# Loading an output projection in 26, 5 and 1 rows instead of 21, 7, 3 and 1, the 26 into another buffer

## The chip, the cores and the metric

The kernel runs on one core of a Trainium2 chip. The core has five engines that run side by side, each with its own instructions in order: PE (matrix multiplication; PEld is its loading of weights), DVE and ACT (elementwise work), POOL, and SP, which here only issues DMA transfers. Transfers bring data from memory (HBM) into the on-chip memory SBUF, which has 128 partitions; PE writes its results to PSUM. The metric is the device time of one execution in microseconds (us), lower is better.

## The reference

Two independent decode steps of attention, A and B, whose results stand side by side in the output. Each has one query token, 32 query heads, 16 key/value heads (two query heads share one), 8192 cached keys, 128 elements a head and a model width of 576. A looks only at its last 2048 keys.

```python
def ref(x, k_cache, v_cache, wq, wo, W):             # A: W = 2048, B: W = 8192
    q = (x @ wq).reshape(B, Sq, Hq, Dh).transpose(0, 2, 1, 3)
    k = repeat(k_cache[:, :, Sk - W:, :], 2, axis=1)
    v = repeat(v_cache[:, :, Sk - W:, :], 2, axis=1)
    scores = einsum("bhqd,bhkd->bhqk", q, k) * Dh ** -0.5
    o = einsum("bhqk,bhkd->bhqd", softmax(scores), v)
    return o.transpose(0, 2, 1, 3).reshape(B, Sq, Hq * Dh) @ wo
out = concatenate([ref(A...), ref(B...)], axis=-1)   # 1152 numbers
```

The caches and the weights are bf16, 102.76 MB are read in all.

## The kernel before

**Order of the work.** The queries of A and B come first: wq of each is loaded and multiplied (`q_part`). Then five groups follow (`NG`): group 0 is the whole of A, groups 1 to 4 are four key/value heads of B each. In each group the keys arrive in two loads (`load_k`, the buffers `("k", 0)` and `("k", 1, ...)`, the first and second quarter of the SBUF tensor `slots`) and the values in one (`load_v`, `("v", 0..2)`, the other half of `slots`). PE turns the keys in eight units (`k_transpose`, line 496), into four PSUM banks. ACT and DVE copy each bank to the SBUF tensor `kt` (lines 506 and 509), which holds four units of 4096 elements per partition; unit u lies in place u mod 4. `k_scores` (line 521) multiplies a unit by the queries, two units behind the transposes. Softmax follows (`softmax_exp`, `softmax_transpose`), then the products with the values (`v_sums`, line 588).

In the last group PE also works out the weights by which the parts of each head are put together (`weights_top`, `weights_exp`, `weights_sum`, `combine`), and A's 4096 results stand ready before the last V sums start. After these, DVE keeps the last group's sums (`v_keep`, line 606), PE combines them (line 671) and DVE copies B's results into `opj` (line 676).

**The output projection.** wo has 4096 x 576 numbers: 32 rows of 576 for each of 128 partitions, so "a row" is here one row in every partition, 144 KB in all. The list `wo_loads` (line 769) says, for A (P = 0) and for B (P = 1), which rows come in which load, to where, and after which buffers are free. `load_wo` makes the load from an entry and `wo_part` (line 691) the matmuls: two per row for A (288 columns each), four per row for B (144 columns each), each of the four in its own strip of 32 columns of the array. All 32 rows of a projection add up in PSUM; `finish_out` copies the sum out and stores it, A's before B's.

**What orders the work.** Each operation names what it reads and writes; `Program.add` notes which earlier operations it must follow, and `emit` turns that into semaphore waits on the engine that runs it. On PE the five groups are a loop; on the other engines they are written out. All loads of slots are issued by SP (line 398 for wo and wq, 407 and 411 for keys, 422 and 427 for values) in program order: one that waits holds all behind it. So before the change SP issues, at the end, A's 32 rows (when the first part of the keys of group 4 has been turned), B's 21 rows (second part of the keys), B's 7 rows (after the last V sums, whose home they take), then 3 and 1 rows behind them, in the same home. The names `("w", 0)` and `("w", 1)` in those two entries are not used elsewhere: they are ordered by standing behind the 7 rows on SP.

PE works through A's 32 rows, then through B's parts in the order of the list, each after its load has landed.

## Time and profile before

| what | value |
|---|---|
| median of the runs | 245.51 us (245.44 to 245.77, 4 runs) |
| the profiled execution, its own time | 245.32 us |
| its span, first to last instruction | 243.8 us |
| read from memory | 102.76 MB, 421 GB/s over the span |
| busy time | PE 161.7 us, PEld 115.9, DVE 88.1, ACT 92.4, POOL 6.4 |
| granted TensorE clock, mean | 0.865 |
| wo of A: issued, landing after | 211.27 us, 19.7 us |
| wo of B, 21 rows: issued, landing after | 211.65 us, 26.5 us |
| wo of B, 7, 3 and 1 rows: landing after | 9.4, 10.1 and 10.0 us |

Times of a place in the profile are counted from the start of the span. "Landing after" is the time from the issue of a load to its last byte. The clock is the share of its full rate that PE was granted; it is 1.00 or 0.50 at any one time. The DMA share is the mean busy share of the core's 16 DMA engines.

### The profile page before, as it was taken

To read this page: it belongs to the slowest core of one execution; us is meant where nothing else is said; L and a number is where in the kernel's file an instruction comes from. 1 tells how busy PE (TensorE), PEld (TensorE's weight loads), DVE (VectorE), ACT (ScalarE), POOL (GpSimd) and SP (SyncE) were. 2 spreads that over 40 slices of the span, in tenths; PEclk is the share of its full clock that TensorE was granted. 3 is DMA by queue.
4 is the path that set the end of the run, shared out by engine and by line. 5 is a ranking of instruction groups with operands and counts; after the bars stand their busy time and mean duration, and the time that the engine had idled before them with its cause. 6 is when DMAs were issued, how large, how long until landed. Compare 5 with 4: busy or idle time off the path is not lost. (4 is left out here: it accounts for less than half of the span.)

```text
span 243.8 us, 5212 instructions
## 1 busy us (share of the span) xinstructions
PE 161.7 (66%) x2325; PEld 115.9 (48%) x2325; DVE 88.1 (36%) x152; ACT 92.4 (38%) x96; POOL 6.4 (3%) x33
## 2 busy tenths in 40 slices
PE   0007639948387995194999453999446699845964
PEld 0002238735236783143886221868222687535753
DVE  0001228854307454203656202555322255533130
ACT  2000017845306686101878300877500387630000
POOL 5000100000000000000000000000000000000000
PEclk9999958997859999657999759999858799977799
DMA  9999999999999999899999999999999999989994
GB/s 339 436 411 419 430 433 422 430 427 430 460 427 431 484 398 462 371 430 435 485 409 452 403 409 430 430 478 430 441 392 430 430 478 430 473 356 441 414 410 179
DMA packets 4064, 102.88 MB, mean 422 GB/s; under 512 B 596, under 2 KB 728, under 8 KB 984
## 3 DMA queue, kind: packets, MB, share of 16 engines
q1 hardware_dynamic: 3896, 102.76, 98.3%
q8 instruction: 6, 0.10, 0.2%
q10 hardware_dynamic: 160, 0.00, 0.0%
q14 instruction: 2, 0.02, 0.0%
HBM read 102.76 MB, written 0.00 MB: 421 GB/s over the span
## 5 line engine op out<-in xcount | busy, mean ns | idle before, releaser
L506 ACT ACTIVATE kt<-ktps 128x1024 bf16<-128x1024 bf16 x80 | 78.9, 1039 | 87.9 <-PE ktps L496 87.9
L496 PE MATMUL ktps<-ident,slots 128*128 128x128 bf16 x1280 | 83.3, 227 | 22.7 <-PEq L214 18.9
L496 PEld LDWEIGHTS ktps<-ident,slots 128*128 128x128 bf16 x1280 | 77.1, 102 | 38.7 <-issue 38.6
L509 DVE COPY kt<-ktps 128x1024 bf16<-128x1024 bf16 x80 | 60.7, 772 | 55.2 <-PE ktps L496 55.2
L588 PE MATMUL opsum<-slots,ptm 128*32 128x512 bf16 x320 | 28.4, 531 | 11.6 <-PEq L214 11.6
L521 PE MATMUL sacc<-kt,qst 128*32 128x512 bf16 x320 | 25.8, 398 | 2.2 <-PEq L214 2.2
L588 PEld LDWEIGHTS opsum<-slots,ptm 128*32 128x32 bf16 x320 | 13.9, 128 | 24.6 <-issue 22.3
L559 PE MATMUL misc<-ident,psb 128*128 128x128 bf16 x40 | 4.5, 283 | 15.8 <-PEq L214 15.8
L606 DVE TENSOR_TENSOR vtmp<-opsum,maskV 128x512 f32<-128x512 f32 x4 | 2.8, 691 | 31.9 <-PE opsum L588 31.9
L547 ACT ACTIVATE psb<-sacc,stat 128x2048 bf16<-128x2048 f32 x5 | 9.8, 1967 | 9.7 <-DVE stat L536 9.7
L559 PEld LDWEIGHTS misc<-ident,psb 128*128 128x128 bf16 x40 | 3.4, 126 | 18.2 <-issue 18.2
L438 PE MATMUL misc<-xnine,twice 64*128 64x18 bf16 x1 | 0.2, 171 | 17.8 <-DMA xnine<-in_B_x_dram 17.8
L566 DVE TENSOR_TENSOR ptm<-misc,maskP 128x1024 bf16<-128x1024 bf16 x5 | 3.5, 691 | 15.9 <-PE misc L559 15.9
L521 PEld LDWEIGHTS sacc<-kt,qst 128*32 128x32 bf16 x320 | 5.0, 94 | 8.4 <-issue 4.8
L438 PEld LDWEIGHTS misc<-xnine,twice 64*128 64x128 bf16 x1 | 0.1, 102 | 17.8 <-issue 17.8
L703 ACT ACTIVATE outsb<-ktps 64x144 bf16<-64x144 f32 x1 | 0.3, 288 | 21.5 <-PE ktps L691 21.5
L691 PE MATMUL ktps<-slots,opj 128*32 128x144 bf16 (+1 forms) x192 | 6.8, 247 | 2.3 <-DMA slots<-in_B_wo_dram 2.3
L462 ACT ACTIVATE qrow<-opsum 128x512 bf16<-128x512 f32 x1 | 0.6, 597 | 19.2 <-PE opsum L456 19.2
L691 PEld LDWEIGHTS ktps<-slots,opj 128*32 128x32 bf16 x192 | 5.2, 97 | 3.8 <-DMA slots<-in_B_wo_dram 3.2
L447 DVE TENSOR_SCALAR xpad<-misc,par 128x5 bf16<-128x5 f32 (+1 forms) x8 | 1.2, 227 | 13.5 <-PE misc L438 13.5
L481 POOL COPY qst<-qcol 128x32 bf16<-128x32 bf16 x8 | 1.7, 213 | 146.3 <-PE sacc L521 146.3
L534 DVE TENSOR_REDUCE stat<-sacc 128x1 f32<-128x512 f32 x5 | 3.5, 691 | 4.4 <-PE sacc L521 4.4
(76 smaller groups left out, 57.7 us busy)
## 6 DMA issues: line engine op xcount, KB each, us to landing
slots<-in_B_k_cache_dram SPq DMA_DIRECT2D x8, 4096.0 KB
slots<-in_A_k_cache_dram SPq DMA_DIRECT2D x4, 2048.0 KB
slots<-in_A_v_cache_dram SPq DMA_DIRECT2D x4, 2048.0 KB
slots<-in_A_wq_dram SPq DMA_DIRECT2D x1, 4608.0 KB, 13.6
slots<-in_B_wq_dram SPq DMA_DIRECT2D x1, 4608.0 KB, 23.8
slots<-in_A_wo_dram SPq DMA_DIRECT2D x1, 4608.0 KB, 19.7
slots<-in_B_wo_dram SPq DMA_DIRECT2D x1, 3024.0 KB, 26.5
slots<-in_B_wo_dram SPq DMA_DIRECT2D x1, 1008.0 KB, 9.4
```

Source lines behind the costliest of these rows:

```text
L481: return pool.tensor_copy(dst, src)
L496: ins = pe.matmul(ktps_bf[q][:, t * 128:(t + 1) * 128], lhsT=slots[:, o:o + 128], rhs=ident[:, :], start=True, stop=True, is_transpose=True)
L506: add("act", lambda act, src=src, dst=dst: act.activation(dst, src, ACT.Copy), reads=[("bank", q)], writes=[("kt", u % NKT, q)], tag="e%d% ...
L509: add("dve", lambda dve, src=src, dst=dst: dve.tensor_copy(dst, src), reads=[("bank", q)], writes=[("kt", u % NKT, q)], tag="e%d%d" % (u, q))
L521: ins = pe.matmul(sacc[32 * j:32 * j + 32, :], lhsT=qst[:, o:o + 32], rhs=rhs, start=(u == 0 and e == 0), stop=True, skip_group_check=True)
L534: add("dve", lambda dve: dve.tensor_reduce(st(C_M + g), sacc[:, :], AX.X, ALU.max), reads=[B_S], writes=[("st", C_M + g)], tag="max")
L547: return act.activation(dst, src, ACT.Exp, bias=st(C_NB + g), scale=SCALE, accum_out=st(C_L + g))
L559: ins = pe.matmul(dst[:, t * 128:(t + 1) * 128], lhsT=psb[:, o:o + 128], rhs=ident[:, :], start=True, stop=True, is_transpose=True)
L566: return dve.tensor_tensor(ptm[:, c * 1024:(c + 1) * 1024].rearrange("p (t y) -> p t y", t=8), dst.rearrange("p (t y) -> p t y", t=8), mas ...
L588: ins = pe.matmul(opsum[64 * j + 32 * x:64 * j + 32 * x + 32, :], lhsT=ptm[:, o:o + 32], rhs=v[:, at[0], at[1], :, :, b:b + 128], start=(n ...
L606: add("dve", lambda dve: dve.tensor_tensor(vtmp[:, :, :], src, by, ALU.mult), reads=[B_O, w], writes=["vtmp"], tag="keep")
L691: ins = pe.matmul(ktps[P + j // 2][32 * j:32 * j + 32, 0:w], lhsT=opj[:, P, at:at + 32], rhs=slots[:, o:o + w], start=(jj == 0), stop=(jj ...
```

## The change

B's wo comes in three loads instead of four. Its first 26 rows go to `kt`, and wait until all four units there have been read by the last scores; the next 5 go to where the 21 rows began, in the second keys' home; the last row follows them there. `load_wo` and `wo_part` take the tensor as an argument. A's load, the order of PE's matmuls and the stores are as they were.

```diff
+    ktw = kt[:, :, :].rearrange("p u y -> p (u y)")
...
-    def load_wo(P, lo, n, off, res):
-        load(slots[:, off:off + n * DM], lambda: wos[P].rearrange("(p j) n -> p (j n)", p=128)[:, lo * DM:(lo + n) * DM],
+    def load_wo(P, lo, n, tile, off, res):
+        load(tile[:, off:off + n * DM], lambda: wos[P].rearrange("(p j) n -> p (j n)", p=128)[:, lo * DM:(lo + n) * DM],
              res, "wo%d_%d" % (P, lo))
...
-                                    rhs=slots[:, o:o + w], start=(jj == 0), stop=(jj == HQ - 1))
+                                    rhs=tile[:, o:o + w], start=(jj == 0), stop=(jj == HQ - 1))
...
     wo_loads = [
-        (0, 0, 32, 0, [("k", 0), ("k", 1, 0)]),
-        (1, 0, 21, WQ_W, [("k", 1, 1)]),
-        (1, 21, 7, 2 * SLOT, [("v", 0), ("v", 1)]),
-        (1, 28, 3, 2 * SLOT + 7 * DM, [("w", 0)]),
-        (1, 31, 1, 2 * SLOT + 10 * DM, [("w", 1)])]
+        (0, 0, 32, slots, 0, [("k", 0), ("k", 1, 0)]),
+        (1, 0, 26, ktw, 0, [("kt", u, q) for u in range(NKT) for q in range(4)]),
+        (1, 26, 5, slots, WQ_W, [("k", 1, 1)]),
+        (1, 31, 1, slots, WQ_W + 5 * DM, [("w", 0)])]
```

## The prediction

> **What bounds the kernel now.** I read the chain of waits first, because it says what ended last. It ends in a wo load, the last rows of B's output projection, the copy out of PSUM and the store:

> ```profile
> 231.53 10.11 DMA slots<-in_B_wo_dram
> 241.64 0.04 issue
> 241.69 0.65 PE ktps L691 x16
> 242.35 0.30 DVE outsb L703
> ```

> Then the list of DMA issues, for how long each wo load took from its issue to its last byte:

> ```profile
> slots<-in_A_wo_dram SPq DMA_DIRECT2D x1, 4608.0 KB, 19.7
> slots<-in_B_wo_dram SPq DMA_DIRECT2D x1, 3024.0 KB, 26.5
> slots<-in_B_wo_dram SPq DMA_DIRECT2D x1, 1008.0 KB, 9.4
> slots<-in_B_wo_dram SPq DMA_DIRECT2D x1, 432.0 KB, 10.1
> slots<-in_B_wo_dram SPq DMA_DIRECT2D x1, 144.0 KB, 10.0
> ```

> The 144 KB load needs as long as the 1008 KB load: all five stand in one line and are served in the order of issue. So I asked for PE's timeline at the end (start, length, line, count, idle time before):

> ```profile
> 233.25 3.96 PE L691 MATMUL ktps<-slots,opj 128*32 128x288 bf16 x62
> 238.21 1.50 PE L691 MATMUL ktps<-slots,opj 128*32 128x144 bf16 x84 [0.99 <-DMA slots<-in_B_wo_dram]
> 240.62 0.62 PE L691 MATMUL ktps<-slots,opj 128*32 128x144 bf16 x28 [0.92 <-DMA slots<-in_B_wo_dram]
> 241.69 0.62 PE L691 MATMUL ktps<-slots,opj 128*32 128x144 bf16 x16 [0.44 <-DMA slots<-in_B_wo_dram]
> ```

> PE starts 0.05 us after a landing (241.64 to 241.69), so the 21, 7 and 3 rows land at 238.16, 240.57 and 241.64; the last row's four matmuls start at 242.05, so it lands at 242.00. A's wo lands at 211.27 + 19.7 = 231.0. PE waits for DMA before every part of B: bytes bound this stage.

> **The change, part by part.**

> *The wait that goes.* The 7, 3 and 1 rows were issued only after the last V sums, at 231.16 to 232. Did the DMA engines run dry meanwhile? In three windows (length; busy time and count of PE, PEld, DVE, ACT, POOL; PE clock; DMA share; GB/s) they did not:

> ```profile
> 228.00:231.00 3.00, 3.00 (x48) 2.38 (x40) 0.00 (x0) 0.00 (x0) 0.00 (x0) 0.82 0.85 364
> 231.00:234.00 3.00, 1.17 (x28) 0.91 (x26) 1.90 (x3) 0.00 (x0) 0.00 (x0) 1.00 0.99 427
> 234.00:237.00 3.00, 3.00 (x54) 2.44 (x48) 0.00 (x0) 0.00 (x0) 0.00 (x0) 1.00 0.97 411
> ```

> The 21 rows were in flight until 238.16, 6 us beyond the last issue. Gain: 0.

> *The wait that is added.* SP now holds the 26 rows until the last scores of group 4 have read kt. That wait ends near 212.8 instead of the 211.65 at which the 21 rows were issued. Behind it on SP stand the two smaller loads and the output stores (first at 237.74). A's 4.6 MB, ahead in line, take about 11 us at the 430 GB/s of the page, so they start near 220 and end at 231; anything issued before that is in time. Cost 0 with 15 us of cover. PE waits on three landings instead of four; those instructions do not show. The other kt accesses are finished by then.

> *The bytes.* The 21 rows took 238.16 - 231.0 = 7.16 us (341 ns a row), the 7 rows 2.41 (344), the 3 rows 1.07 (357), the last 0.36. So 26 rows take 26 x 0.341 = 8.87 and land at **239.87**; 5 rows at 344 to 357 ns take 1.72 to 1.79 and land at 241.6 to 241.65; the last row lands at 241.95 to 242.0. One load fewer saves at most 0.05 us.

> *The work behind the bytes.* This is what moves. 21 rows now start at 238.21 and are done by 239.7, before the next landing. With the change nothing of B can start until 239.87 + 0.05 = **239.92**. Then 31 rows are owed. 84 matmuls in 1.50 us, less 0.23 for the last one's length, are 1.27 / 20 = 63 ns a row (four matmuls side by side). 31 rows take 31 x 0.063 = 1.95 us, until 241.87; row 31 starts at 242.05 as now. At full clock the end doesn't move, with 0.18 us to spare.

> *The clock under that work.* PE now idles from about 237.05 (its last column of A's rows) to 239.92: 2.87 us instead of 0.99. Here I asked for windows 3.41 us long, placed on the edges at which the granted clock changes (length, PE busy and count, clock, DMA share, GB/s):

> ```profile
> 147.16:150.57 3.41, 1.41 (x28) 1.00 1.05 452
> 150.57:153.99 3.42, 1.62 (x30) 1.00 0.98 422
> 171.05:174.47 3.42, 1.53 (x23) 1.00 1.06 460
> 174.47:177.88 3.41, 1.76 (x16) 0.50 0.98 423
> ...
> 235.91:239.32 3.41, 2.42 (x94) 1.00 0.93 383
> ```

> The clock holds for a whole window and follows the work of the window before: 1.53 us busy at 171.05 is followed by 0.50, 1.41 at 147.16 by 1.00. The busy column includes each burst's drain. Counting only columns that stream (512 columns in 0.21 us at full clock), the first is 1.04 us (31%) and the second 1.23 (36%). So a full clock is lost below roughly a third of a window. The next row of this kernel's end, 235.91 to 239.32, would keep only 237.05 - 235.91 = 1.14 us (33%) of streaming after the change: the very edge. And the edges do not sit still against the work: after the last scores the clock fell 1.5 us later in the group before the last and 2.6 us later in the last (scores end 172.96 and 212.81, clock falls 174.47 and 215.43). So I move the edge e through one window and price each place, with 63 ns a row at 1.00 and twice that, 126 ns, at 0.50:
> - e = 239.5: cold until 242.91, 23.7 rows; the other 8.3 take 0.52: end 243.43, against 242.11 now: +1.3 us.
> - e = 239.9: 27 rows cold, 5 warm: end 243.6, +1.5.
> - e = 240.5: 9.2 rows warm, 22.8 x 0.126 = 2.87: end 243.37, +1.3.
> - e = 241.0: 17 warm, 15 cold: end 242.87, +0.8.
> - From 241.1 to 242.7, which are the same places as 237.7 to 239.3: the window keeps a third; the end stays.

> The drop needs 2.2 to 2.35 us of idle time in a window, so e lies between 239.3 and 241.1: half of all places. Where V sums ran at 1.00 throughout (here the first 3.3 us ran at 0.50), A's rows end up to 1.7 us earlier, and some more places lose. I take 55%. Before, the same gate has nothing to bite on: with 0.99, 0.92 and 0.44 us of idle time and at most 21 rows per landing, even 126 ns a row ends 21 rows at 240.9 and the next 7 at 241.7, so the end would move by 0.1.

> [...]

> **Sum.** Bytes 0 to -0.05, waits 0, catch-up at full clock 0, clock 0 to +1.5. The profiled execution took 245.32 us (span 243.8), 0.19 under the median of 245.51. A reported time is a median over executions with different edges: the middle over all places is about +0.6, over the losing ones +1.3. I take **+0.9**: 246.2 for such an execution, 246.4 as a median.

> **Rivals.**
> 1. *The clock stays up* (the other side). If the work before 237.05 counts for more than a third of the window, or most executions have a favourable edge, 31 rows fit between 239.92 and 242.05. It decides at the spare 0.18 us: three cold rows. Time 245.45 to 245.55. For it: 33% lies between a row that lost the clock and one that kept it. Against: half the places are clear losses.
> 2. *PE's code comes late.* In the middle of the transposes PE once idled 3.83 us for "issue" (51.71 to 55.54) with its data there, and the profile lists six 16 KB instruction transfers. One burst of 31 rows could run into such a gap that a DMA wait now covers. Bounds: 0 to 3.8 us, the latter 249. Against: the same 192 matmuls stand in the same order, and none of their gaps shows "issue" now. I take 0.
> 3. *It gains.* If the last issues did starve some DMA engines, or three larger loads ran faster than the rows per load above, up to 0.5 us: 245.0. Against: shares of 0.97 and 0.99.

> **How the numbers follow.** Clock lost in most executions 0.57 (0.53 slower by over 0.2%, that is 0.49 us, about what a measurement can tell from no change; 0.04 within), clock kept 0.35, late code 0.04, gain 0.04. So slower 0.57, same 0.39, faster 0.04. The range runs from the kept clock with 0.15 of scatter, 245.3, to the dearest edge, 245.5 + 1.5 = 247.0; the likeliest case alone has 246.0 to 247.0.

> **What would show it.** Right: the 26 rows start near 239.9, idle over 2 us before them, 104 matmuls at more than 1.6 us, a clock of 0.50 somewhere in 239.3 to 242.9, the last matmul after 242.8. Wrong: the same landings with 1.00 throughout and the last row near 242.05 (rival 1); a gap "issue" among the last rows (2); the last landing clearly before 241.9 (3). If the 26 rows landed later than 240, the bytes were mis-priced.

## The result and the profile after

The changed kernel takes 245.56 us (median of 51 runs, 245.20 to 247.44), the kernel before 245.47 us (median of 72 runs, 245.22 to 245.78). The ratio is 1.002, with a 95% interval of 1.0012 to 1.0028.

The median hides most of it. The 51 times fall into two heaps with nothing between them: 33 from 245.20 to 245.73 (mean 245.48, as before) and 18 from 246.57 to 247.44 (mean 246.96). The change costs either nothing or 1.5 us; 18 of 51 times 1.5 us is the 0.2% of the ratio. None of the 72 runs before lies above 245.78. (The kernel before was timed again beside the experiments; each ratio below is against the runs of its own round, and none of those 75 lies above 245.95.)

The profiled execution is one of the upper heap: 246.91 us, span 245.5. Its chain of waits still holds a landing, that of the 26 rows, but with much more of PE behind it (start, length, what; ktps is where PE adds up the rows, outsb the copy that is stored):

```profile
213.34 27.03 DMA kt<-in_B_wo_dram
240.37 0.04 issue
240.41 3.60 PE ktps L692 x121
244.01 0.02 issue
244.04 0.30 DVE outsb L704
```

Before, the last piece of PE ahead of the copy was 0.65 us long, now it is 3.60. The list of DMA issues and PE's timeline show the same from both sides:

```profile
slots<-in_A_wo_dram SPq DMA_DIRECT2D x1, 4608.0 KB, 19.7
kt<-in_B_wo_dram SPq DMA_DIRECT2D x1, 3744.0 KB, 27.0
slots<-in_B_wo_dram SPq DMA_DIRECT2D x1, 720.0 KB, 28.4
slots<-in_B_wo_dram SPq DMA_DIRECT2D x1, 144.0 KB, 28.2
```

```profile
233.81 3.96 PE L692 MATMUL ktps<-slots,opj 128*32 128x288 bf16 x62
...
240.41 3.19 PE L692 MATMUL ktps<-kt,opj 128*32 128x144 bf16 x104 [2.64 <-DMA kt<-in_B_wo_dram]
243.44 0.54 PE L692 MATMUL ktps<-slots,opj 128*32 128x144 bf16 x24
```

This execution runs about half a microsecond later than the one profiled before: A's wo is issued at 211.76 and lands at 231.46. From there the 26 rows take 240.37 - 231.46 = 8.91 us. The 5 and 1 rows had landed when PE came to them at 243.44: there is no wait in front of the 24 matmuls. The 104 matmuls take 3.19 us, where 84 took 1.50 before: 29 ns each against 15.

Why they are slow stands in the windows between the edges of the granted clock (length, PE busy and count, clock, DMA share, GB/s):

```profile
229.69:233.10 3.41, 1.99 (x36) 1.00 0.96 413
233.10:236.52 3.42, 3.00 (x56) 1.00 1.04 447
236.52:239.93 3.41, 1.25 (x22) 1.00 0.86 352
239.93:243.34 3.41, 2.93 (x100) 0.50 0.25 93
```

The window 236.52 to 239.93 holds the end of A's rows and then nothing; the next has half the clock, and in it fall the rows of B. Before, the 21 rows of B began at 238.21, and the window of that place (235.91 to 239.32) was busy for 2.42 us.

### The profile page after: what moved, and what is told of

Same layout as the page of the kernel before. It is cut to its first block, busy times and chain, and to the rows that moved or that the text cites. A ratio compares the mean times of both kernels' runs of the same rounds, so it can differ in the third digit from the quotient of the medians.

```text
span 245.5 us, 5211 instructions
## 1 busy us (share of the span) xinstructions
PE 165.3 (67%) x2325; PEld 119.9 (49%) x2325; DVE 88.3 (36%) x152; ACT 92.8 (38%) x96; POOL 6.3 (3%) x33
## 5 line engine op out<-in xcount | busy, mean ns | idle before, releaser
L497 PE MATMUL ktps<-ident,slots 128*128 128x128 bf16 x1280 | 85.8, 231 | 22.0 <-PEq L214 17.9
L497 PEld LDWEIGHTS ktps<-ident,slots 128*128 128x128 bf16 x1280 | 79.7, 104 | 37.8 <-issue 37.8
L692 PE MATMUL ktps<-kt,opj 128*32 128x144 bf16 x104 | 3.2, 320 | 2.6 <-DMA kt<-in_B_wo_dram 2.6
L560 PE MATMUL turned<-ident,psb 128*128 128x128 bf16 x40 | 4.8, 295 | 0.0
## 6 DMA issues: line engine op xcount, KB each, us to landing
slots<-in_A_wq_dram SPq DMA_DIRECT2D x1, 4608.0 KB, 13.8
slots<-in_B_wq_dram SPq DMA_DIRECT2D x1, 4608.0 KB, 24.0
slots<-in_A_wo_dram SPq DMA_DIRECT2D x1, 4608.0 KB, 19.7
```

Of the source, the lines that this page charges most:

```text
L497: ins = pe.matmul(ktps_bf[q][:, t * 128:(t + 1) * 128], lhsT=slots[:, o:o + 128], rhs=ident[:, :], start=True, stop=True, is_transpose=True)
L560: ins = pe.matmul(dst[:, t * 128:(t + 1) * 128], lhsT=psb[:, o:o + 128], rhs=ident[:, :], start=True, stop=True, is_transpose=True)
L692: ins = pe.matmul(ktps[P + j // 2][32 * j:32 * j + 32, 0:w], lhsT=opj[:, P, at:at + 32], rhs=tile[:, o:o + w], start=(jj == 0), stop=(jj = ...
```

## The experiments

The theory: PE's gap before the 26 rows costs it the full clock in those executions in which a window of 3.41 us falls badly on it, and 26 rows at half clock end late. The rival: the new load itself is late in some executions, for its home or SP's new wait, and PE only follows. Further rivals stand with single runs. Where nothing else is said, a kernel differs from the changed one in what its diff shows. "The upper heap" is the times from 246.57 up.

### The gap filled

```diff
+    def filler(n):
+        def mm(pe):
+            for i in range(n):
+                ins = pe.matmul(sacc[:, :], lhsT=ident[:, :], rhs=psb[:, 512 * (i % 4):512 * (i % 4) + 512], start=True, stop=True)
+            return ins
+        add("pe", mm, reads=["ident", "psb"], writes=[B_S])
...
         finish_out(P)
+        if P == 0:
+            filler(8)
```

> The changed kernel, with eight matmuls of 512 columns on PE between A's rows and B's rows, whose sums nobody reads (about 1.7 us at full clock, into the idle time of 2.6 to 2.9 us). Theory (the clock): PE's idle time costs it the full clock in those executions whose 3.41 us window falls badly, and 26 rows at half clock end late. With the gap filled the clock stays at 1.00 and every execution takes 245.2 to 245.8, median 245.5; the third that took 246.6 to 247.4 is gone. Rival (the transfer): in a third of the executions the 26 rows land late, for their destination or for SP's new wait. Then the filler changes nothing and a third stays at 246.6 to 247.4.

Measured: 245.54 us median of 11 runs, ratio 0.9996 (0.9987 to 1.0005). Nine lie from 245.31 to 245.62, two at 246.01 and 246.09; none is at 246.57 or above. The upper heap is gone with the loads untouched: against the rival. The two late ones were not expected, and the profiled execution is one of them:

```profile
235.25 3.96 PE L692 MATMUL ktps<-slots,opj 128*32 128x288 bf16 x62
239.37 1.67 PE L774 MATMUL sacc<-psb,ident 128*128 128x512 bf16 x7 [0.16 <-issue]
240.98 1.81 PE L692 MATMUL ktps<-kt,opj 128*32 128x144 bf16 x104
```

Here A's rows ended only at 239.2, so the filler itself stood in the way of the 26 rows, which start with no wait for DMA in front of them. (The other late run has no trace.) That A's rows can be that late turned out to matter.

### The split undone, the home and the missing wait kept

```diff
-        (1, 0, 26, ktw, 0, [("kt", u, q) for u in range(NKT) for q in range(4)]),
-        (1, 26, 5, slots, WQ_W, [("k", 1, 1)]),
-        (1, 31, 1, slots, WQ_W + 5 * DM, [("w", 0)])]
+        (1, 0, 21, ktw, 0, [("kt", u, q) for u in range(NKT) for q in range(4)]),
+        (1, 21, 7, ktw, 21 * DM, [("w", 1)]),
+        (1, 28, 3, slots, WQ_W, [("k", 1, 1)]),
+        (1, 31, 1, slots, WQ_W + 3 * DM, [("w", 0)])]
```

> Undoes the split alone: B's rows come in 21, 7, 3 and 1 again, but the 21 and the 7 go to kt behind the last scores, and the 3 and 1 follow at once; nothing waits for the V sums. Theory (the clock): PE starts at 238.2 again, the gap is 1 us, and the work owed at each landing is short: all executions at 245.2 to 245.8, median 245.45, no gain over the kernel before since the DMA engines never ran dry there. Rival (the transfer): destination and wait are those of the changed kernel, so a third stays at 246.6 to 247.4. Rival (it gains): 245.0 or less, if the wait for the V sums did cost bytes.

Measured: 245.57 us median of 11 (245.38 to 245.81), ratio 1.0000 (0.9991 to 1.0009). No upper heap: neither kt as a home nor SP's wait for the last scores is to blame. And there is no gain from dropping the wait for the V sums: it cost nothing before.

### The V wait put back, the 26 rows kept

```diff
-        (1, 26, 5, slots, WQ_W, [("k", 1, 1)]),
-        (1, 31, 1, slots, WQ_W + 5 * DM, [("w", 0)])]
+        (1, 26, 5, slots, 2 * SLOT, [("v", 0), ("v", 1)]),
+        (1, 31, 1, slots, 2 * SLOT + 5 * DM, [("w", 0)])]
```

> The changed kernel, but the 5 and the 1 rows go to the home of the values again and so wait for the last V sums on SP; the 26 stay in kt. This undoes the other part of the change alone. Theory (the clock): the wait is hidden by the 26 rows in flight until 240, so the two kinds of executions remain, 245.2 to 245.8 and 246.5 to 247.5, with a quarter to a half in the upper one; median 245.5 to 246.6. In the trace, slow if the clock comes back during the V sums before 230.3 and not slow otherwise. Rival (the wait for the V sums matters): with it put back all executions are as before, 245.2 to 245.8.

Measured: four runs from 245.46 to 245.72, six from 246.62 to 246.99; median 246.68, ratio 1.0040 (1.0025 to 1.0054). Both heaps are there, at the same places. Six of ten is somewhat more than the quarter to a half expected, as ten runs may give; the median jumps because it falls in the other heap. With the two experiments before, this leaves the size of the first load as the part that counts.

### A larger first load

```diff
+        (1, 0, 28, ktw, 0, [("kt", u, q) for u in range(NKT) for q in range(4)]),
+        (1, 28, 3, slots, WQ_W, [("k", 1, 1)]),
+        (1, 31, 1, slots, WQ_W + 3 * DM, [("w", 0)])]
```

> More of the same: 28, 3 and 1 rows, the 28 in kt. Theory (the clock): the 28 rows land near 240.55, PE idles 3.5 us, so nearly every place of the window loses the clock; 28 rows at 126 ns are 3.5 us and the end moves by about 2 us in most executions (247.2 to 247.8), by 0.4 to 0.5 us where the clock stays (28 x 0.063 = 1.76 us from 240.6, then 4 rows): median near 247. Rival (the transfer): one load of 28 rows is no worse than one of 26: median 245.56 with a third at 246.6 to 247.4.

Measured: 247.32 us median of 7 (245.92, 246.40, 246.76, then four from 247.32 to 247.88), ratio 1.0055 (1.0036 to 1.0074). As the theory had it: even the best is 0.3 us over the median before, 245.59 in this round. The profiled one has 2.26 us of idle time, 112 matmuls in 3.49 us, and these windows:

```profile
237.56:240.97 3.41, 1.15 (x26) 1.00 0.64 252
240.97:244.38 3.41, 3.41 (x124) 0.50 0.07 25
```

### The gap kept, half of the catch-up left out

```diff
             for jj in range(lo, lo + n):
+                if P and 0 < jj < 14:
+                    continue
```

> The changed kernel with 13 of the 26 rows of B's first part left out of the matmuls (the loads are all there; the output of B lacks those rows). Theory (the clock): the gap and the loss of the clock stay, but 13 + 5 rows at half clock are 18 x 0.126 = 2.3 us from 239.9, ending at 242.2 instead of 243.6: at most 0.2 us late, so all executions at 245.2 to 245.9, with a clock of 0.50 among the last rows where the window falls badly. Rival (the transfer): the late landing remains, a third at 246.0 or more.

Measured: 245.62 us median of 11 (245.28 to 245.94), ratio 1.0002 (0.9993 to 1.0011). The kernel leaves out the matmuls of 13 of the 26 rows. The clock was lost in the profiled execution, of 245.82 us, all the same:

```profile
236.78:240.19 3.41, 1.05 (x18) 1.00 0.79 319
240.19:243.61 3.42, 2.63 (x76) 0.50 0.15 60
```

So it is not the lost clock that costs, but the lost clock with 104 matmuls still owed.

### What decides: three repeats for their traces

The traces so far suggested a relation, and it was put to the test on three more executions of the changed kernel, with no edit. E is the time at which the clock comes back to 1.00 during the last V sums.

> The changed kernel once more, for its trace. Theory: let E be the time at which the clock comes back to 1.00 during the V sums. A's rows then end near E + 8.1 and the third window edge after E is E + 10.24. If E is under about 230.3, that window holds only the 1.1 to 1.2 us of A's rows, the clock falls to 0.50 before or as the 26 rows start, and the last matmul ends after 243.4. If E is later, the first rows of B count into the window, it keeps over 36%, and the last matmul ends near 242.8. Rival (chance or the transfer): no such order by E.

> The changed kernel once more, for its trace: as for the first repeat, slow with E under 230.3, not slow with E above it.

> The changed kernel once more, for its trace: as for the first repeat, slow with E under 230.3, not slow with E above it.

Measured: E = 230.68, 229.59 and 231.01; 245.48, 246.83 and 245.46 us. All three fell on the side that was said, though the last matmul of the two in the lower heap ended at 242.5 and not near 242.8. Windows of the second repeat, which is in the upper heap, and then of the third, which is not:

```profile
236.42:239.83 3.41, 1.08 (x18) 1.00 0.88 361
239.83:243.25 3.42, 3.08 (x104) 0.50 0.27 102
```

```profile
227.59:231.01 3.42, 3.42 (x46) 0.50 1.00 428
...
237.83:241.25 3.42, 2.43 (x94) 1.00 0.73 290
```

In the third, V sums ran at 0.50 until 231.01, so A's rows ended at 239.13 and the gap was only 0.99 us; the window that covers it also holds B's first rows. All traces in which 26 rows with all their matmuls follow an empty gap; the last row is of the next experiment:

| kernel | E | A's rows end | B's rows start | clock at B's rows | last matmul ends | its time |
|---|---|---|---|---|---|---|
| V-wait put back | 230.62 | 238.51 | 240.24 | 1.00 | 242.53 | 245.46 |
| first repeat | 230.68 | 238.53 | 240.15 | 1.00 | 242.46 | 245.48 |
| third repeat | 231.01 | 239.13 | 240.12 | 1.00 | 242.53 | 245.46 |
| second repeat | 229.59 | 237.50 | 240.17 | 0.50 from 239.83 | 243.80 | 246.83 |
| changed kernel | 229.69 | 237.77 | 240.41 | 0.50 from 239.93 | 243.98 | 246.91 |
| filler before the V sums | 228.45 | 237.37 | 240.32 | 1.00 | 242.64 | 245.57 |

### The V sums meant to run faster

```diff
             weights_top(g)
+            filler(2, (g, 19.05, LAST))
             weights_exp(g)
+            filler(1, (g, 19.15, LAST))
             weights_sum(g)
+            filler(3, (g, 19.25, LAST))
```

> The changed kernel, with six matmuls of 512 columns whose sums nobody reads (2, 1 and 3) in the three gaps that PE has while the head weights are worked out, ahead of combine and the V sums. They do not touch the end of the kernel. Theory (the clock): PE's busy windows there bring the full clock back before the V sums, these end near 229 instead of 231 to 233, A's rows near 235.5, and PE then idles 4.5 us before the 26 rows, in which any window of 3.41 us falls under 36% of streaming. So the clock is lost in nearly every execution: median near 247.0, almost all from 246.5 to 247.5. Faster V sums make a slower kernel. Rival (the filler before A's rows does nothing; chance alone decides): median 245.56 with a third above 246.5, as in the changed kernel.

Measured: 245.57 us median of 12, nine from 245.42 to 245.89 and three from 246.97 to 247.21; ratio 1.0017 (1.0001 to 1.0033). The expectation fell, because its condition wasn't met: the filler didn't bring the clock back.

```profile
218.21:221.62 3.41, 2.87 (x11) 0.50 0.90 389
221.62:225.04 3.42, 3.19 (x12) 0.50 1.05 453
225.04:228.45 3.41, 3.41 (x48) 0.50 0.95 411
...
235.28:238.69 3.41, 2.09 (x35) 1.00 0.96 408
```

Busy 2.87 and 3.19 us of 3.41, and yet 0.50 stayed: the busy column counts small f32 matmuls by their whole length (two of one column each, at 219.88, by 0.58 us). Counted by columns that stream (the last section says how), these windows hold an estimated 32% and 40%: two and three matmuls of the filler at 0.427 us each, and the columns of the f32 matmuls. So the times say nothing for or against the theory.

The trace says something. The clock came back at 228.45, the earliest of all twelve traces, and PE idled longer than in the changed kernel's trace, yet kept 1.00:

```profile
240.32 1.81 PE L692 MATMUL ktps<-kt,opj 128*32 128x144 bf16 x104 [2.95 <-DMA kt<-in_B_wo_dram]
```

The edge at 238.69 cuts the gap in two: the window before it holds A's last rows, the next one, to 242.11, B's first (an estimated 56% and 50% by columns that stream: 1.9 us of A's rows after 235.28, 1.7 us of B's after 240.32). So "E under 230.3 is slow" holds on one side only. Among traces with 26 rows loaded and nothing put into the gap, the clock fell with E from 229.59 to 230.01 and stayed with 228.45 and from 230.62 on. What sorts them is the work in each window, not the length of the gap.

### Less work ahead of the gap

So the gap was lengthened in another way:

```diff
             for jj in range(lo, lo + n):
+                if not P and 0 < jj < 17:
+                    continue
```

> The changed kernel with 16 of A's 32 rows left out of the matmuls (the output of A lacks those rows): PE has 2 us less to do ahead of the gap, which the loads do not notice. Theory (the clock): A's rows now end near E + 6.1, E being the time at which the clock comes back during the V sums, so the window that ends at E + 10.24 holds none of them and keeps its 36% only where B's rows have run for 1.24 us in it, that is for E over about 231.2 instead of 230.3. So less work makes a slower kernel: 6 to 10 of 11 executions above 245.9 instead of some 4, the empty stretch between 245.8 and 246.5 gets some of them, median 246.3 to 247.0. Rival (the catch-up alone matters, or chance): as the changed kernel, about 4 of 11 above 246.5, median 245.6.

Measured: 246.93 us median of 8, one at 245.53 and seven from 246.63 to 247.38; ratio 1.0048 (1.0031 to 1.0064). Leaving out the matmuls of 16 of A's rows puts seven of eight executions into the upper heap, where the changed kernel had 18 of 51, as the theory said and the rival did not. The part on the empty stretch was wrong: no run lies between 245.8 and 246.5. The windows of the profiled one, with a gap of 4.39 us:

```profile
233.42:236.83 3.41, 2.29 (x40) 1.00 1.00 430
236.83:240.25 3.42, 0.00 (x0) 1.00 0.87 354
240.25:243.66 3.41, 2.99 (x104) 0.50 0.17 67
```

No kernel here beats the kernel before: all end on the same bytes, and what PE does behind them is at best hidden.

## Why the prediction was right and where it was wrong

**Right: the bytes.** 26 rows were priced at 8.87 us after A's wo and took 8.91 in the profiled execution. The wait that goes gained 0 and the wait that comes cost 0, as the runs with 21 rows in kt and with the V wait put back show.

**Right: the catch-up at full clock.** 104 matmuls take 1.81 us in the first and third repeat, and the last matmul ends at 242.46 and 242.53, near the 242.30 of before. Rival 1 (the clock stays up) is what happens in the lower heap.

**Right: the clock.** Idle time of 2.64 us took the full clock away, and the price was +1.3 to +1.5 for most places; the upper heap lies 1.5 us above the lower one. The length of the gap alone does not decide it: gaps of 2.26, 2.64 and 2.67 us cost the clock (the run with 28 rows, the changed kernel and its second repeat), while one of 2.95 did not (the filler before the V sums).

**Wrong: how often.** The forecast was 246.4, on the clock being lost in most executions. The median is 245.56, in the range but in the case that had 0.35; the range covered both heaps, so that it holds the median shows little. The step that went wrong is the share of losing places: "Where V sums ran at 1.00 throughout [...], A's rows end up to 1.7 us earlier, and some more places lose. I take 55%". In none of the twelve traces did V sums run at 1.00 throughout: the clock came back between 228.45 and 231.34, 1.8 to 3.9 us after their first matmul. And the places before that, "e lies between 239.3 and 241.1", came from moving the edge along a gap that stood still at 2.87 us. In truth a later edge means V sums at half clock for longer (before, four of their matmuls start every 0.427 us at 0.50 and every 0.216 us at 1.00), so A's rows end later and the gap shrinks: in the first and third repeat and with the V wait put back A's rows end at 238.5 to 239.1 and the gap is 0.99 to 1.73 us. At edges of 240.86 and 240.91, which the prediction counted as lost, the clock stayed. The place "e = 241.0, +0.8" stayed empty as well: no run of the changed kernel lies between 245.73 and 246.57. In 51 runs the share is 35%; with the repeats and the run with the V wait put back it is 25 of 64, 39%. With two heaps 1.5 us apart, a share under one half puts the median at no change, and one over it at more than 1 us.

**Not seen.** A gap "issue" in the midst of the last rows (rival 2, late code) stands in no trace, and nothing gained (rival 3).

What stays open: how the edges fall in a given execution was read from each trace, not set by an experiment. So the share of the upper heap was counted, not derived.

## What to carry to other kernels

A load that is merged to save a transfer lets its matmuls start later and all at once: price the idle time before and the burst after it together, since the one may take the clock from the other (here 2.64 us of idle time, then 104 matmuls in 3.19 us instead of 1.81). Where an engine's clock changes at the edges of windows that lie elsewhere against the work in each execution (here E was 228.45 to 231.34), look at the spread of many executions and not at the median alone; a change may cost 1.5 us in a third of them and show as 0.1. And when you move such a window along the work, let the work before it move too.

## What the runs showed of the hardware that was not expected

Elsewhere the busy time does not sort so well: in the kernel before, 1.53 us at 171.05 was followed by 0.50 and 1.41 us at 147.16 by 1.00. An estimate of the columns that stream does better. It counts each matmul's columns from its start, overlaps once, at the pace of the V sums in the trace of the kernel before, where four matmuls of 512 columns side by side start every 0.216 us at 1.00 and every 0.427 us at 0.50. In the traces of the kernel before and of the changed kernel, 83 windows that start at 1.00 after the first 30 us can be followed into the next. The 20 with 0% to 35% by this estimate were followed by 0.50, the 63 with 36% or more by 1.00; the nearest two are 34.7% (the changed kernel at 147.77) and 36.5% (the kernel before at 147.16). That is what these two traces hold, and no limit was set by an experiment.

At 0.50 the same work did not bring the full clock back. In the kernel before, 1.76 us of busy PE at 174.47, 2.45 at 222.25 and 2.54 at 65.24 were followed by 0.50, while 2.81 at 215.43 and 3.41 at 225.67 were followed by 1.00. With the filler before the V sums, 2.87 us at 218.21 and 3.19 at 221.62 were followed by 0.50.

An engine that is far from being the bottleneck sets the time here by working too little: with half of A's matmuls left out the kernel takes 0.48% more than the kernel before, where the changed kernel takes 0.20% more.
